# Values of the first two token blocks taken from raw x, with mean and scale applied on the way out

## The chip, the core and the metric

The kernel runs on one core of a Trainium2 chip. The metric is the device time of one execution in microseconds (us); it is given as the median of several executions. Engines are named as in the profile: PE is TensorE (PEld its weight loads), DVE is VectorE, ACT is ScalarE, POOL is GpSimd, SP is SyncE, whose queue here only issues DMAs.

## What is computed

A layer norm of x (2048 tokens, 512 features), then two branches on the normalised tokens, added to x: a sliding-window attention (32 heads of 16, window 256) and a bilinear feed-forward of width 1792.

```python
x = A_x
xn = (x - mean(x)) / sqrt(var(x) + 1e-5)
q, k, v = split(xn @ wqkv)                      # 32 heads of 16
scores = q @ k.T / 4, masked to 0 <= i - j < 256
attn = softmax(scores) @ v @ wo
mlp = ((xn @ w_gate) * (xn @ w_up)) @ w_down
return x + attn + mlp
```

All inputs and the output are bfloat16.

## The kernel before

The tokens are cut into 4 chunks (T = 0 to 3) of 512, and each chunk into 4 blocks (b) of 128. Everything stays in SBUF: the weights are loaded once at the start, and only x comes in and the result goes out.

The order of all engines' instructions is written by a planner inside the kernel, when the program is built. `run` keeps a clock for TensorE (`now`) and one for each other engine (`free`). Steps of VectorE, ScalarE and GpSimd are `op`s with a duration for each engine that may do them, a list of what they wait for, and a rank. TensorE's work is a list `A` of dense groups (four products of one bank of PSUM, mostly), a list `B` of down projections, the score batches (76 of them), and the value groups of the attention (16). `choose` takes among the first four entries of `A` (`WINDOW`) the one that can begin first; a change of tile shape costs `SWITCH`, and a transpose (`turn`) that is due within 0.4 is preferred:

```python
t = max(t, free[0][0], now)
t += SWITCH * (d.mode != self.mode) + SWITCH * (d.mode == "C" and self.mode == "D")
t -= 0.5 * (d.name.startswith("turn") and t <= now + 0.4)
```

Before the first score, an `op` with a rank above zero is held back by `HOLD` against others. Times such as `land`, `wv`, `wk`, `wq` are when a load is expected. These times only decide the order; on the chip each instruction waits for semaphores.

PSUM has eight banks: four (`S`) hold the scores of a batch, four (`M0` to `M3`) rotate among all other products. An evacuation (a copy from PSUM to SBUF) gives its bank back.

The start, chunk 0, is `first_chunk`. The prologue issues the loads on two queues, SP's and ACT's, and 42 filler matmuls (`keep_busy`, L204). For each block the statistics follow on VectorE (L598, L600), the root on ScalarE (L607), the reciprocal (L610) and the normalisation (L280) on VectorE; then TensorE transposes the block (`turn`, L631), an engine copies the transpose to `xnT` (L208 on ScalarE or L210 on VectorE), and keys, queries (L646) and values (L698, `add_v`) are projected from it. The statistics of block 1 are in two halves, the second one after block 0's normalisation. Values of a block are 16 products of 128x256 in two column tiles, one for each lane of 64 tokens. Keys go out in two copies (L291 or L289), queries in one.

After the start, chunks 1 to 3 get their transposes by DMA (L684), while scores (L222), exponentials (L505), masks (L231, L237), attention values (L252) and gate, up, down and output products (L214) alternate on TensorE. The last block's sum is made in two halves of 256 columns (`add_down`): the first goes out on SP's queue, the second, in a bank of `S`, on ACT's.

Of the kernel before, what the change touches and what calls it, by code (L numbers as in the profile page):

```python
# [36 lines left out]
class Dense:  # L37


    def __init__(self, name, mms, deps, emit, evac, mode="D"):  # L40
        self.name, self.mms, self.deps, self.emit, self.evac, self.mode = name, mms, deps, emit, evac, mode


# [43 lines left out]
class Kernel:  # L87
# [2 lines left out]
    PACE = 2.9  # L90
    SHARE = 1.0
    FEED = 0.1
    HOLD = 0.2

    def __init__(self, live=True):
        self.live = live
# [4 lines left out]
    def open(self, ctx, tc, x, wqkv, wo, wg, wu, wd, out):  # L101
        self.tc, self.nc = tc, tc.nc
        self.x_d, self.out_d = x.flatten_outer_dims(), out.flatten_outer_dims()
        self.w_d = dict(qkv=wqkv, o=wo, g=wg, u=wu, d=wd)
        self.F = wg.shape[1]

        def pool(name, bufs, **kw):
            return ctx.enter_context(tc.tile_pool(name=name, bufs=bufs, **kw))

        c = self.const = pool("const", 1)  # L110
        self.work, self.few = pool("work", 3), pool("few", 2)
        psum = pool("psum", 1, space=bass.MemoryType.PSUM)
# [24 lines left out]
        self.eps = c.tile([128, 1], F32, name="eps")  # L137
        self.own = c.tile([128, 2], F32, name="own")
        self.mhalf = c.tile([128, 4], F32, name="mhalf")
        self.masks = c.tile([128, 5, 64], I16, name="masks")  # L140
        self.S = psum.tile([128, 4, 512], F32, name="S")
        self.M = [psum.tile([128, 512], F32, name=f"M{i}") for i in range(4)] + [self.S[:, 3, :]]

    def prologue(self):
        nc = self.nc
# [3 lines left out]
        def load(eng, dst, src):  # L149
            eng.dma_start(out=dst, in_=src)  # L150

        def qkv(eng, lo, k0, k1):
            load(eng, self.Wqkv[:, k0:k1, lo:lo + 512], w["qkv"][:, k0:k1, lo:lo + 512])

        qkv(nc.sync, 1024, 0, 1)
        load(nc.scalar, self.x[:, 0, :], xv[:, 0, :])
        load(nc.sync, self.x[:, 1, :], xv[:, 1, :])
        qkv(nc.scalar, 1024, 2, 4)
        qkv(nc.sync, 1024, 1, 2)
        qkv(nc.scalar, 512, 2, 4)  # L160
        qkv(nc.sync, 512, 0, 2)
        load(nc.sync, self.x[:, 2, :], xv[:, 2, :])
# [6 lines left out]
            if lo == 0:  # L169
                load(nc.sync, self.x[:, 4:8, :], xv[:, 4:8, :])  # L170
        load(nc.sync, self.x[:, 8:NT, :], xv[:, 8:NT, :])
        for f, g in ((0, 7), (7, 14)):
            load(nc.sync, self.Wd[:, f:g], w["d"][:, f:g])
        load(nc.sync, self.Wo[:], w["o"])
        for _ in range(4):
            nc.sync.drain()

        c = self.const
        nc.gpsimd.memset(self.ident[:], 0.0)
# [2 lines left out]
        nc.gpsimd.memset(self.mhalf[:], -0.5)  # L182
        warm = c.tile([128, 1], F32, name="warm")
        nc.vector.memset(warm[:], 0.0)
        nc.vector.memset(self.eps[:], 1e-5)
        nc.scalar.activation(out=warm[:], in_=warm[:], func=ACT.Sqrt)
        self.warm = warm
# [5 lines left out]
        nc.vector.tensor_copy(out=self.own[:, 1:2], in_=podd[:])  # L193
        nc.vector.tensor_scalar(out=self.own[:, 0:1], in0=podd[:], scalar1=0, scalar2=None, op0=ALU.is_equal)
        nc.gpsimd.memset(self.V[0][:, :, :, 16:18], 1.0)
        self.keep_busy(42, 0)

# [80 lines left out]
    def i_apply(self, t, cols=slice(0, 512)):  # L278
        w, b = t // 4 % 2, t % 4
        self.nc.vector.tensor_scalar(out=self.xn[b][:, cols], in0=self.x[:, t, cols], scalar1=self.mv[w][:, b, 0:1],  # L280
                                     scalar2=self.rs[w][:, b:b + 1], op0=ALU.subtract, op1=ALU.mult)

    def i_keys(self, e, T, c, lane, in_, blocks=slice(0, 8)):

# [10 lines left out]
    def run(self):  # L295
        if self.live:
            self.prologue()
        self.now, self.mode = 4.8, "D"
# [127 lines left out]
    def do(self, at, kind, what):  # L426
# [9 lines left out]
            self.do_values(at)  # L436
        elif kind == "DA":
            d = self.A.pop(what)
            i = self.take_bank()
            o = self.pe(at, d.mms * MM, d.name)  # L440
            if self.live:
                d.emit(i)
# [139 lines left out]

    def first_chunk(self):

        land = (3.45, 3.9, 7.2, 9.6)
        wv, wk, wq = 5.4, 6.6, 9.2
        nc = self.nc
        roots = []
        for b in range(4):
# [13 lines left out]
            for n in range(halves):  # L603
# [3 lines left out]
            s = self.op(f"sq{b}", {"A": (0.24, 0.25)}, [s], lambda e, b=b: nc.scalar.activation(  # L607
                out=self.ve[:, b:b + 1], in_=self.mv[0][:, b, 1:2], func=ACT.Sqrt, bias=self.eps[:]), rank=0)
            roots.append(s)
            s = self.op(f"rs{b}", {"V": (0.15, 0.16)}, [s], lambda e, b=b: nc.vector.reciprocal(  # L610
                out=self.rs[0][:, b:b + 1], in_=self.ve[:, b:b + 1]), rank=0)
# [11 lines left out]
        for n in (1, 2):  # L623
            last = self.op("ones", {"G": (0.26, 0.33)}, [last], lambda e, n=n: self.nc.gpsimd.memset(
                self.V[n][:, :, :, 16:18], 1.0), rank=9)
        for b in range(4):
            tok = slice(128 * b, 128 * b + 128)

            def turn(i, ks, b=b):
                for k in ks:  # L630
                    self.nc.tensor.transpose(self.psT(i)[:, k, :], self.xn[b][:, 128 * k:128 * k + 128], self.ident[:])  # L631
                if b == 0:
                    self.keep_busy(2 * ks[0], 3)

            def turned(o, i, ks, b=b, tok=tok):
                took = {"A": (0.48, 0.6), "V": (0.31, 0.41)} if len(ks) == 4 else {"A": (0.27, 0.38)}
# [35 lines left out]
            self.add(f"q0b{b}", 4.4, [("xnT", 0, b), wq], lambda i, f=project: f(i, 0), q_out)  # L672

    def norms(self, T):
        w = T % 2
# [14 lines left out]
    def add_v(self, T, b, land=0.0):  # L690
# [14 lines left out]
            self.frees(x, i)  # L705
            self.at_["V", T, b] = x

        x = [("xnT", T, b)] if T + b else [("xnT", 0, 0, 0), ("begun", 0, 0, 2)]
# [50 lines left out]
    def add_down(self, T, b):  # L759
# [82 lines left out]
```

The softmax here doesn't subtract the row's maximum and nothing guards it: scores larger than these inputs give would overflow.

## Time and profile before

| | |
|---|---|
| median of 5 executions | 265.86 us (265.63 to 266.27) |
| the profiled execution | 265.63 us |
| its span, first to last instruction | 263.7 us |
| TensorE busy | 256.4 us (97%) |
| VectorE, ScalarE, GpSimd busy | 187.7, 167.7, 119.6 us |
| first value products of block 0 (L698) | 6.34 us after the span's start |
| values of blocks 1 to 3 | from 17.60 us |
| first scores (L222) | 17.27 us |
| last attention values (L252) | 245.18 us |
| last output's DMA issued | 261.22 us |

The busy time of TensorE includes the tail of each product and its overlap with the next, so it is not its rate; the spacing of products is taken from groups of them. A row of the timeline gives start, length, engine, line, operation, and in brackets how long the engine sat idle before it and what ended that.

### The profile page before, as it was taken

The numbers are of one execution on the slowest core, as the hardware profiler recorded it, in microseconds if no ns is written. First come the engines' busy times: TensorE is split into PE (matmuls) and PEld (weight loads), VectorE is DVE, ScalarE is ACT, GpSimd is POOL, SyncE is SP. The second block draws the span as 40 slices with busy tenths as digits, with TensorE's granted clock in tenths as the row PEclk, the third lists the DMA queues.
The fourth block names the chain that finished last, engine by engine and source line by source line (L and its number), as shares of the span: only waits on it lengthen the run. The fifth ranks groups of instructions, "written<-read, shape, count | busy, mean of one in ns | idle before, by whom it ended". The sixth has DMA issues, their size and how long they took to land.

```text
span 263.7 us, 7965 instructions
## 1 busy us (share of the span) xinstructions
PE 256.4 (97%) x3420; PEld 131.9 (50%) x3456; DVE 187.7 (71%) x363; ACT 167.7 (64%) x127; POOL 119.6 (45%) x272
## 2 busy tenths in 40 slices
PE   8999999999999999999999999999999999999995
PEld 7974444553535353465544453536535444544562
DVE  4789886969994438798897548786955449787504
ACT  3777576769677677577777766675786765674000
POOL 1047655455465554618165645437073645427000
PEclk9999999999999999999999999999999999999999
DMA  6999910000004000000002300000000000000002
GB/s 214 380 374 349 222 23 1 2 2 1 2 3 102 20 22 24 0 2 2 2 0 53 73 22 20 2 4 0 2 2 22 21 22 22 0 2 0 2 2 81
DMA packets 17251, 13.88 MB, mean 53 GB/s; under 512 B 7104, under 2 KB 17216, under 8 KB 17216
## 3 DMA queue, kind: packets, MB, share of 16 engines
q1 hardware_dynamic: 16384, 12.65, 17.9%
q10 hardware_dynamic: 832, 0.72, 0.9%
q8 instruction: 27, 0.44, 0.7%
q14 instruction: 8, 0.07, 0.1%
HBM read 9.70 MB, written 2.10 MB: 45 GB/s over the span
## 4 chain that ended last, share of the span: by engine, by line
PE 94%; DMA 2%; issue 1%; DVE 1%; ACT 0%
PE M L214 68%; PE S L222 10%; PE M L252 7%; PE M L698 6%; PE M L646 3%; DMA x<-in_A_x_dram 1%; DMA out_dram<-xn 1%; PE M L631 1%; PE S L214 1%; DVE xn L792 1%; DVE st L598 0%; DVE xn L280 0%; ACT ve L607 0%; PE M L204 0%; DVE mv L600 0%
## 5 line engine op out<-in xcount | busy, mean ns | idle before, releaser
L505 ACT ACTIVATE P<-S 128x2048 bf16<-128x2048 f32 x76 | 140.9, 1854 | 56.2 <-PE S L222 48.7
L231 POOL TENSOR_SCALAR_AFFINE_SELECT P<-P 64x256 bf16<-64x256 bf16 (+1 forms) x248 | 112.5, 456 | 106.8 <-ACT P L505 92.2
L214 PE MATMUL M<-xnT,Wg 128*128 128x512 bf16 x219 | 57.4, 380 | 0.3
L214 PE MATMUL M<-xnT,Wu 128*128 128x512 bf16 x213 | 56.6, 380 | 0.4
L214 PE MATMUL M<-Wd,hT 128*128 128x512 bf16 (+1 forms) x214 | 50.2, 373 | 1.4 <-issue 1.3
L750 DVE TENSOR_TENSOR hT<-M,gsb 128x512 bf16<-128x512 f32 x56 | 38.3, 683 | 7.3 <-PE M L214 7.0
L214 PEld LDWEIGHTS <-hT 128*128 128x128 bf16 x238 | 21.6, 98 | 23.2 <-issue 1.9
L214 PEld LDWEIGHTS <-Wg 128*128 128x128 bf16 x224 | 20.5, 98 | 24.9 <-issue 2.3
L210 DVE CAST gsb<-M 128x512 bf16<-128x512 f32 x41 | 28.1, 684 | 6.4 <-PE M L214 6.1
L214 PEld LDWEIGHTS <-Wu 128*128 128x128 bf16 x224 | 20.3, 98 | 24.6 <-issue 2.4
L222 PE MATMUL S<-Q,K 32*128 32x320 bf16 (+3 forms) x720 | 30.0, 254 | 0.3
L541 DVE STREAM_TRANSPOSE at<-M 128x512 f32<-128x512 f32 x32 | 21.4, 699 | 11.9 <-PE M L252 11.9
L237 DVE TENSOR_TENSOR P<-P,masks 128x512 int16<-128x512 int16 x56 | 22.3, 405 | 8.3 <-ACT P L505 8.3
L222 PEld LDWEIGHTS <-K 32*128 32x128 bf16 x720 | 12.0, 92 | 32.3 <-issue 31.1
L214 PE MATMUL M<-xnT,Wqkv 128*128 128x512 bf16 x90 | 22.6, 380 | 0.3
L792 DVE TENSOR_TENSOR y<-M,x 128x512 bf16<-128x512 f32 x12 | 8.3, 688 | 17.8 <-PE M L214 17.6
L252 PE MATMUL M<-P,V 64*17 64x320 bf16 (+4 forms) x1440 | 19.5, 252 | 0.0
L252 PEld LDWEIGHTS <-V 64*17 64x17 bf16 x1440 | 17.1, 86 | 3.0 <-issue 1.1
L291 DVE TENSOR_SCALAR K<-M,own 128x512 bf16<-128x512 f32 x21 | 15.1, 743 | 2.6 <-PE M L214 1.9
L214 PE MATMUL M<-Wo,OT 128*128 128x512 bf16 (+1 forms) x60 | 15.5, 373 | 0.5 <-issue 0.5
L698 PE MATMUL M<-Wqkv,xnT 128*64 128x256 bf16 x256 | 15.5, 274 | 0.0
L698 PEld LDWEIGHTS <-xnT 128*64 128x64 bf16 x256 | 13.4, 110 | 1.9 <-issue 1.6
(53 smaller groups left out, 149.9 us busy)
## 6 DMA issues: line engine op xcount, KB each, us to landing
Wg<-in_B_w_gate_dram SPq DMA_DIRECT2D x2, 896.0 KB, 9.6
Wu<-in_B_w_up_dram SPq DMA_DIRECT2D x2, 896.0 KB, 11.4
Wd<-in_B_w_down_dram SPq DMA_DIRECT2D x2, 896.0 KB, 13.3
out_dram<-y SPq DMA_DIRECT2D x12, 128.0 KB, 1.7
x<-in_A_x_dram SPq DMA_DIRECT2D x1, 1024.0 KB, 13.6
Wqkv<-in_A_wqkv_dram ACTq DMA_DIRECT2D x2, 256.0 KB, 4.4
Wqkv<-in_A_wqkv_dram SPq DMA_DIRECT2D x1, 512.0 KB, 5.4
x<-in_A_x_dram SPq DMA_DIRECT2D x1, 512.0 KB, 10.4
```

Source lines behind the costliest of these rows:

```text
L210: self.nc.vector.tensor_copy(out=out, in_=in_)
L214: self.nc.tensor.matmul(ps, lhsT=a, rhs=b, start=first and n == 0, stop=last and n == len(pairs) - 1)
L222: self.nc.tensor.matmul(self.S[:, e, 64 * at:64 * (at + m)], lhsT=self.K[U % 3][rows, c, j].rearrange("p l t -> p (l t)"), rhs=self.Q[T % ...
L231: self.nc.gpsimd.affine_select(out=v, in_=v, pattern=[[0, 4], [0, n], [sign, 64]], base=0, fill=0.0, compare_op=ALU.is_gt if kind else ALU ...
L237: self.nc.vector.tensor_tensor(out=v, in0=v, in1=m, op=ALU.bitwise_and)
L252: self.nc.tensor.matmul(banks[lane][32 * e:32 * e + 17, 64 * q:64 * (q + m)], lhsT=self.V[U % 3][rows, j, 4 * c + e, 0:17], rhs=P[rows, e, ...
L291: self.nc.vector.tensor_scalar(out=out, in0=in_, scalar1=own, scalar2=None, op0=ALU.mult)
L505: ex = self.op(f"exp{g}", {"A": (took + 0.06, took + 0.18)}, [o], lambda e: self.nc.scalar.activation(out=P[:, :, 0:hi], in_=self.S[:, :, ...
L541: t = self.op(f"tr{v}", {"V": (0.63, 0.71)}, [o] + ts, lambda e, par=par: nc.vector.transpose(out=self.at[:, :, par, :], in_=self.M[banks[ ...
L698: self.nc.tensor.matmul(self.M[i][64 * lane:64 * lane + 64, 256 * jj:256 * jj + 256], lhsT=self.xnT[T % 2][:, k, tok], rhs=w[:, lane], sta ...
L750: x = self.op(f"u{T}.{f}", {"V": PSUM_COPY["V"]}, [o, ("gate", T, f)], lambda e: self.nc.vector.tensor_tensor(out=self.hT[T % 2][:, f, :], ...
L792: self.nc.vector.tensor_tensor(out=keep["y"][:, cols], in0=self.M[i][:, cols], in1=self.x[:, t, cols], op=ALU.add)
```

## The change

1. Blocks 0 and 1 of x are transposed as they are loaded (`raw0`, `raw1`), into banks of `S`, with 2 and 14 filler matmuls behind them. ScalarE or VectorE copies the transposes to `xnT[1]`, which is free until chunk 1. Three of the four copies come after block 0's root on ScalarE.
2. Products of this raw x with the value weights (32 of them) go into two banks of `S`; products of a tile of -1 with the value weights (8 of them) give minus the column sums in a third one. They come in two parts of 20, `v01a` for the first half of the features and `v01b` for the second.
3. Later, at a low rank, the column sums are copied to SBUF, mean and reciprocal root are copied to the partitions of each lane (`rj`), VectorE adds mean times minus the column sum (`scalar_tensor_tensor`), and ScalarE multiplies by the reciprocal root into `V[0]`.
4. Values of blocks 0 and 1 are no longer projected from normalised tokens. Keys of chunk 0 wait for the start of `v01b`; the first scores wait for these values, as they use the same banks. Block 0's transposes lose their filler.
5. The reciprocal root is written over the variance. `HOLD` is 0.3 in place of 0.2, the planner's clock starts at 3.6 in place of 4.8, and 27 fillers stand in place of 42.
6. Loads: block 1 of x comes first on SP's queue; the first half of the value weights is one load instead of two; `Wd` is loaded in three pieces instead of two. Two drains on SP and four on VectorE take the place of four on SP.
7. The last block's sum is split into 320 and 192 columns instead of 256 and 256.

```diff
-        self.M = [psum.tile([128, 512], F32, name=f"M{i}") for i in range(4)] + [self.S[:, 3, :]]
+        self.M = [psum.tile([128, 512], F32, name=f"M{i}") for i in range(4)] + [self.S[:, e, :] for e in (3, 0, 1, 2)]
...
-        qkv(nc.sync, 1024, 0, 1)
         load(nc.scalar, self.x[:, 0, :], xv[:, 0, :])
         load(nc.sync, self.x[:, 1, :], xv[:, 1, :])
+        qkv(nc.sync, 1024, 0, 2)
         qkv(nc.scalar, 1024, 2, 4)
-        qkv(nc.sync, 1024, 1, 2)
...
-        for f, g in ((0, 7), (7, 14)):
+        for f, g in ((0, 5), (5, 10), (10, 14)):
             load(nc.sync, self.Wd[:, f:g], w["d"][:, f:g])
         load(nc.sync, self.Wo[:], w["o"])
+        for _ in range(2):
+            nc.sync.drain()
         for _ in range(4):
-            nc.sync.drain()
+            nc.vector.drain()
...
+        nc.gpsimd.memset(self.minus[:], -1.0)
...
-        self.keep_busy(42, 0)
+        self.keep_busy(27, 0)
...
-        deps = {("S", g - 1), ("Pfree", g - self.PBUFS)}
+        deps = {("S", g - 1), ("Pfree", g - self.PBUFS)} | ({("raw values", 0), ("raw values", 1)} if g == 0 else set())
...
-        land = (3.45, 3.9, 7.2, 9.6)
-        wv, wk, wq = 5.4, 6.6, 9.2
+        land = (3.5, 3.5, 7.6, 9.6)
+        wv, wk, wq = 5.4, 7.1, 9.2
...
-            at = len(self.A) - 2 if b else 0
+            at = len(self.A) - 2 if b else 3
...
-            self.add_v(0, b, wv)
-            self.add(f"k0b{b}", 4.4, [("xnT", 0, b), wk], lambda i, f=project: f(i, 512), k_out)
+            if b > 1:
+                self.add_v(0, b, wv)
+            self.add(f"k0b{b}", 4.4, [("xnT", 0, b), wk, ("values",)], lambda i, f=project: f(i, 512), k_out)
...
-            halves = [(slice(0, 256), {}, MM / 2), (slice(256, 512), {"bank": 4}, MM / 2)]
+            halves = [(slice(0, 320), {}, MM * 0.625), (slice(320, 512), {"bank": 4}, MM * 0.375)]
```

The new function, called from `first_chunk` ahead of its loop over blocks:

```python
def first_values(self, land, wv):
    raw = self.xnT[1]
    csum = self.P[6].bitcast(F32)[:, 0, :]
    vraw = self.at.rearrange("p a b c -> p (a b c)")
    for b in range(2):
        tok = slice(128 * b, 128 * b + 128)

        def turn(i, b=b):
            for k in range(4):
                nc.tensor.transpose(self.psT(i)[:, k, :], self.x[:, b, 128 * k:128 * k + 128], self.ident[:])
            self.keep_busy((2, 14)[b], 3)

        def turned(o, i, b=b, tok=tok):
            for n in range(2):
                ks = slice(2 * n, 2 * n + 2)
                deps = [o] + ([("sq", 0)] if b + n else [])
                self.at_["raw", b, n] = self.op(f"raw{b}", {"A": (0.27, 0.38), "V": (0.20, 0.29)}, deps, lambda e, ks=ks: self.copy(
                    e, raw[:, ks, tok], self.psT(i)[:, ks]), rank=0.2)

        self.add(f"raw{b}", 1.1, [land[b]], turn, turned, "D", 4 + b)

    def emit(i, ks):
        W = self.Wqkv[:, :, 1024:1536].rearrange("p k (h l d) -> p k l h d", l=2, d=16)
        for k in ks:
            for lane in range(2):
                nc.tensor.matmul(self.M[4][64 * lane:64 * lane + 64, 0:256], lhsT=self.minus[:], rhs=W[:, k, lane], ...)
        for b in range(2):
            for k in ks:
                for jj in range(2):
                    tok = slice(128 * b + 64 * jj, 128 * b + 64 * jj + 64)
                    for lane in range(2):
                        nc.tensor.matmul(self.M[6 + b][64 * lane:64 * lane + 64, 256 * jj:256 * jj + 256],
                                         lhsT=raw[:, k, tok], rhs=W[:, k, lane], ...)

    def evac(o, i):
        self.at_["values",] = o.start
        late = ("xnT", 0, 2)
        c = self.op("csum", {"V": (0.33, 0.41), "A": (0.3, 0.38)}, [o, late], lambda e: self.copy(
            e, csum, self.M[4][:, 0:256]), rank=5)
        for b in range(2):
            def stats(e, b=b):
                for j in range(2):
                    for lane in range(2):
                        self.copy(e, self.rj[b][64 * lane:64 * lane + 64, j, :], self.mv[0][64 * j:64 * j + 64, b, :])

            r = self.op(f"rj{b}", {"V": (0.5, 0.55), "A": (0.8, 0.85)}, [("rs", b), late], stats, rank=5)
            x = c
            for j in range(2):
                x = self.op(f"vm{b}", {"V": (0.36, 0.42)}, [c, r, x], ...)   # vraw = csum * mean + products
                v = self.op(f"V0.{b}", {"A": (0.32, 0.4)}, [x], ...)         # V[0] = vraw * reciprocal root
            self.at_["V", 0, b] = self.at_["raw values", b] = v

    raws = [("raw", 0, 0), ("raw", 0, 1), ("raw", 1, 0)]
    self.add("v01a", 4.9, raws + [wv - 0.35], lambda i: emit(i, (0, 1)), lambda o, i: self.at_.update({("v01a",): 0.0}), "C", 4)
    self.add("v01b", 4.9, [("raw", 1, 1), wv, ("v01a",)], lambda i: emit(i, (2, 3)), evac, "C", 4)
```

More of the change, by code (lines that the diff above doesn't have):

```diff
@@ L37, with __init__ @@
 class Dense:
-    def __init__(self, name, mms, deps, emit, evac, mode="D"):
+    def __init__(self, name, mms, deps, emit, evac, mode="D", bank=None):
+        self.bank = bank
         self.name, self.mms, self.deps, self.emit, self.evac, self.mode = name, mms, deps, emit, evac, mode
@@ L92 @@
     FEED = 0.1
-    HOLD = 0.2
+    HOLD = 0.3
     def __init__(self, live=True):
@@ L141, in open @@
         self.S = psum.tile([128, 4, 512], F32, name="S")
-        self.M = [psum.tile([128, 512], F32, name=f"M{i}") for i in range(4)] + [self.S[:, 3, :]]
+        self.M = [psum.tile([128, 512], F32, name=f"M{i}") for i in range(4)] + [self.S[:, e, :] for e in (3, 0, 1, 2)]
+        self.rj = some("rj", 2, [128, 2, 2], F32)
+        self.minus = c.tile([128, 64], BF16, name="minus")
     def prologue(self):
@@ L280, in i_apply @@
         self.nc.vector.tensor_scalar(out=self.xn[b][:, cols], in0=self.x[:, t, cols], scalar1=self.mv[w][:, b, 0:1],
[L281 removed]
+                                     scalar2=self.rs[w][:, b:b + 1] if t > 3 else self.mv[0][:, b, 1:2], op0=ALU.subtract, op1=ALU.mult)
     def i_keys(self, e, T, c, lane, in_, blocks=slice(0, 8)):
@@ L297, in run @@
             self.prologue()
-        self.now, self.mode = 4.8, "D"
+        self.now, self.mode = 3.6, "D"
         self.free = {"V": 3.0, "A": 3.4, "G": 3.0, "S": 6.0}
@@ L438, in do @@
             d = self.A.pop(what)
-            i = self.take_bank()
+            i = self.take_bank() if d.bank is None else d.bank
             o = self.pe(at, d.mms * MM, d.name)
@@ L609, in first_chunk @@
             roots.append(s)
+            self.at_["sq", b] = s
             s = self.op(f"rs{b}", {"V": (0.15, 0.16)}, [s], lambda e, b=b: nc.vector.reciprocal(
-                out=self.rs[0][:, b:b + 1], in_=self.ve[:, b:b + 1]), rank=0)
+                out=self.mv[0][:, b, 1:2], in_=self.ve[:, b:b + 1]), rank=0)
+            self.at_["rs", b] = s
             parts = 2 if b == 0 else 1
@@ L625, in first_chunk @@
                 self.V[n][:, :, :, 16:18], 1.0), rank=9)
+        self.first_values(land, wv)
         for b in range(4):
@@ L631, in turn @@
                     self.nc.tensor.transpose(self.psT(i)[:, k, :], self.xn[b][:, 128 * k:128 * k + 128], self.ident[:])
-                if b == 0:
-                    self.keep_busy(2 * ks[0], 3)
             def turned(o, i, ks, b=b, tok=tok):
-                took = {"A": (0.48, 0.6), "V": (0.31, 0.41)} if len(ks) == 4 else {"A": (0.27, 0.38)}
+                took = {"A": (0.48, 0.6), "V": (0.31, 0.41)} if len(ks) == 4 else {"A": (0.27, 0.38), "V": (0.20, 0.29)}
                 ks = slice(ks[0], ks[-1] + 1)
@@ L669, in first_chunk, with evac @@
                                             lambda o, i, f=turned, ks=ks: f(o, i, ks)))
-            self.add_v(0, b, wv)
-            self.add(f"k0b{b}", 4.4, [("xnT", 0, b), wk], lambda i, f=project: f(i, 512), k_out)
+            if b > 1:
+                self.add_v(0, b, wv)
+            self.add(f"k0b{b}", 4.4, [("xnT", 0, b), wk, ("values",)], lambda i, f=project: f(i, 512), k_out)
             self.add(f"q0b{b}", 4.4, [("xnT", 0, b), wq], lambda i, f=project: f(i, 0), q_out)
+    def first_values(self, land, wv):
+        nc = self.nc
+        if self.live:
+            raw = self.xnT[1]
+            csum = self.P[6].bitcast(F32)[:, 0, :]
+            vraw = self.at.rearrange("p a b c -> p (a b c)")
+        for b in range(2):
+            tok = slice(128 * b, 128 * b + 128)
+            def turn(i, b=b):
+                for k in range(4):
+                    nc.tensor.transpose(self.psT(i)[:, k, :], self.x[:, b, 128 * k:128 * k + 128], self.ident[:])
[9 more added lines that the diff above has]
+            W = self.Wqkv[:, :, 1024:1536].rearrange("p k (h l d) -> p k l h d", l=2, d=16)
+            for k in ks:
+                for lane in range(2):
+                    nc.tensor.matmul(self.M[4][64 * lane:64 * lane + 64, 0:256], lhsT=self.minus[:], rhs=W[:, k, lane],
+                                     start=k == 0, stop=k == 3, tile_position=(0, 64 * lane), skip_group_check=True)
+            for b in range(2):
+                for k in ks:
+                    for jj in range(2):
+                        tok = slice(128 * b + 64 * jj, 128 * b + 64 * jj + 64)
+                        for lane in range(2):
+                            nc.tensor.matmul(self.M[6 + b][64 * lane:64 * lane + 64, 256 * jj:256 * jj + 256],
+                                             lhsT=raw[:, k, tok], rhs=W[:, k, lane], start=k + jj == 0, stop=k + jj == 4,
+                                             tile_position=(0, 64 * lane), skip_group_check=True)
+        def evac(o, i):
+            self.at_["values",] = o.start
[5 more added lines that the diff above has]
+                    for j in range(2):
+                        for lane in range(2):
+                            self.copy(e, self.rj[b][64 * lane:64 * lane + 64, j, :], self.mv[0][64 * j:64 * j + 64, b, :])
+                r = self.op(f"rj{b}", {"V": (0.5, 0.55), "A": (0.8, 0.85)}, [("rs", b), late], stats, rank=5)
+                x = c
+                for j in range(2):
+                    cols = slice(256 * j, 256 * j + 256)
+                    x = self.op(f"vm{b}", {"V": (0.36, 0.42)}, [c, r, x], lambda e, b=b, j=j, cols=cols: nc.vector.scalar_tensor_tensor(
+                        out=vraw[:, 512 * b + 256 * j:512 * b + 256 * j + 256], in0=csum, scalar=self.rj[b][:, j, 0:1], in1=self.M[6 + b][:, cols],
+                        op0=ALU.mult, op1=ALU.add), rank=5)
+                    v = self.op(f"V0.{b}", {"A": (0.32, 0.4)}, [x], lambda e, b=b, j=j, cols=cols: nc.scalar.activation(
+                        out=self.V[0][:, 2 * b + j, :, 0:16], in_=vraw[:, 512 * b + 256 * j:512 * b + 256 * j + 256].rearrange("p (h d) -> p h d", d=16),
+                        func=ACT.Copy, scale=self.rj[b][:, j, 1:2]), rank=5)
+                self.at_["V", 0, b] = self.at_["raw values", b] = v
+        raws = [("raw", 0, 0), ("raw", 0, 1), ("raw", 1, 0)]
+        self.add("v01a", 4.9, raws + [wv - 0.35], lambda i: emit(i, (0, 1)), lambda o, i: self.at_.update({("v01a",): 0.0}), "C", 4)
+        self.add("v01b", 4.9, [("raw", 1, 1), wv, ("v01a",)], lambda i: emit(i, (2, 3)), evac, "C", 4)
@@ L706, in evac @@
             self.at_["V", T, b] = x
-        x = [("xnT", T, b)] if T + b else [("xnT", 0, 0, 0), ("begun", 0, 0, 2)]
+        x = [("xnT", T, b)]
         self.add(f"v{T}.{b}", 4, x + [land] + self.ring(T, 2)[:1 if T == 3 else 0], emit, evac, "C")
```

## The prediction

> **What bounds the kernel now.** I read the page first (busy shares and the chain that ended last), then that chain in order of time for the first 16 us, then the timeline of the start, the turn into attention and the end, and last the busy times by stretch.
>
> ```profile
> span 263.7 us, 7965 instructions
> ...
> PE 256.4 (97%) x3420; PEld 131.9 (50%) x3456; DVE 187.7 (71%) x363; ACT 167.7 (64%) x127; POOL 119.6 (45%) x272
> ...
> PE 94%; DMA 2%; issue 1%; DVE 1%; ACT 0%
> ```
>
> TensorE is busy for 97% of the span and makes 94% of the chain. So only three things can move the time: how much TensorE has to do, how early it starts without a pause, and what follows its last product. The chain's first steps show where the unbroken stretch begins:
>
> ```profile
> 3.70 0.71 DVE st L598
> ...
> 5.17 0.36 DVE xn L280
> ...
> 5.58 0.54 PE M L631 x4
> 6.12 0.23 PE M L204 x4
> 6.35 1.05 PE M L698 x16
> 7.40 0.04 issue
> 7.45 0.40 PE M L631 x4
> 7.84 1.79 PE M L646 x32
> ```
>
> L631 is a transpose of normalised tokens, L698 the values, L646 keys and queries, L204 filler. Before 7.45 us TensorE does only block 0's transposes and values that anyone needs; from 7.45 on it hardly stops. What starts the stretch, and where the other values lie, is in the timeline:
>
> ```profile
> 0.84 4.64 PE L204 MATMUL M<-const-bfloat16-1.0 128*128 128x128 bf16 x42 [0.84 <-PEq L826]
> ...
> 6.97 0.41 DVE L280 TENSOR_SCALAR xn<-x,mv,rs 128x512 bf16<-128x512 bf16 x1
> ...
> 7.44 0.23 PEld L631 LDWEIGHTS <-xn 128*128 128x128 bf16 x4 [0.31 <-DVE xn L280]
> ...
> 9.63 0.23 PEld L631 LDWEIGHTS <-xn 128*128 128x128 bf16 x4 [0.17 <-DVE xn L280]
> ...
> 17.60 2.81 PE L698 MATMUL M<-Wqkv,xnT 128*64 128x256 bf16 x48
> ```
>
> Block 1's transpose waits for VectorE's normalisation of block 1 (6.97), block 2's for 0.17 us. Values of blocks 1 to 3 are 48 products in one go at 17.60.
>
> **Front, the main term.** *Removed:* 16 of those 48 products. Groups of 48 take 2.74 in the chain, groups of 32 1.87 (at 116.45): 0.87 us off the path. *Added on TensorE:* 8 transposes of raw x; 32 products of raw x and 8 of the column of -1, in two parts of 20. One product costs (2.81-0.27)/47 = 0.054, so a part is 1.08; 48 by 0.054 make 2.59 and the chain has 2.74, so changing tile shape costs about 0.1, entering or leaving.
>
> Which part is free depends on the order, which the planner writes. I followed its rules for the first steps by hand, for order only. Raw transposes come first, then block 0's two half transposes, then part one, as its copies are due. Then a transpose due within 0.4 us is preferred by 0.5: block 1's lies about 0.03 inside that limit, so it goes ahead of part two; and keys of block 0 are made to wait for part two's start. On the chip:
>
> - Part one. 27 fillers at 0.107 end at 3.7, about when x lands (3.68, where the statistics start at 3.70). Two raw transposes with 16 fillers are 24 matrices more. The copies of raw x are four ScalarE steps of 128x256 (0.38 each, the row of xnT<-M 128x256), in ScalarE's waits of 0.89 and 0.96 before 4.65 and 5.90; the third ends near 5.6. Part one starts about 6.1 and ends about 7.2, still inside the wait for block 1: free.
> - Block 1's transposes: its chain of statistics is untouched, so 7.45 again.
> - Part two follows: 0.1 + 1.08 + 0.1 = 1.28 before block 0's keys, which started right after this transpose before.
> - Block 2's wait of 0.17 disappears, as its norm gets 1.28 more.
>
> Front: +1.28 - 0.87 - 0.16 = **+0.25 us**. A part of 20 with two changes of shape takes the place of 16 in a group that stays. If the hand-followed margin of 0.03 is wrong, part two goes first: 6.13 + 2.16 = 8.3, transposes till 8.6, keys at 8.6 instead of 7.67: +0.95 - 0.87 - 0.16 = -0.1.
>
> **The clock.** The 42 fillers come every 0.107 us to 5.2, the keys every 1.79/32 = 0.056 from 7.7; so the array runs at half speed for the first 4.5 us, though the granted clock is printed as 1.00 there. By this trace the 24 matrices end near 5.9 (about 15 at 0.107, the rest at 0.056). The Trainium skill, "TensorE: Matmul & The Clock Gate", Part 1, says that full speed is granted after a busy window of about 3.4 us that runs free, so that the moment varies from run to run. From work at 0.84 that puts it anywhere up to 0.84+6.8 = 7.7 (estimate from that page). The rule speaks against the change: its early work is real, 20 products now stand where 16 stood, and in that worst case the 24 matrices end at 6.3, block 0's transposes at 6.7, and part one, by the page at half speed until 7.7, at about 8.3 in place of 7.45: +0.85. By the row it costs 0. I take +0.1, the bounds being -0.2 (steadier filling helps every run) and +0.85.
>
> **VectorE and ScalarE before the first score.**
>
> ```profile
> 9.60:12.00 2.40, 2.40 (x44) 2.37 (x44) 1.97 (x5) 2.22 (x5) 0.00 (x0) 1.00 1.06 391
> 12.00:14.00 2.00, 2.00 (x40) 2.00 (x37) 1.69 (x4) 1.27 (x3) 0.98 (x5) 1.00 1.06 370
> 14.00:16.00 2.00, 1.95 (x31) 1.75 (x30) 1.46 (x3) 1.97 (x4) 1.70 (x8) 1.00 1.08 367
> ```
>
> Columns three and four after the stretch's length are TensorE and its loads, then VectorE and ScalarE. From 9.6 to 16 VectorE idles 1.28 and ScalarE 0.94 us. The change adds here: one copy of the column sums (0.42, the row y-sum 128x256 of f32), eight tiny copies of mean and scale (0.15 alone by the 128x1 CAST, 0.07 apart in a row: 0.6 to 1.2), four multiply-adds of 128x256 (no row; 0.42 by that nearest row, 0.35 to 0.7 each), and on ScalarE four scaled copies (0.38 each): about 4.4 us. Removed are a ScalarE copy of 0.60 and a later VectorE one of 0.68. TensorE's own delay of 1.28 gives both engines together 2.5 us, so 1.9 are left for gaps of 2.2, in fragments. They stand at the lowest rank, but where an engine has begun one, a key or query copy behind it waits up to 0.4, its bank of four comes free later, and TensorE waits for that. Bounds: 0, and 1.9/2 = 0.95 if no fragment can be used. I take +0.2, nearer to 0, because four banks carry 0.9 each.
>
> The first score now also waits for these values. It was at 17.27 and may come at 18 to 19; gate and up products cover that as long as banks are free. At the other end 9.03 + 2.97 us of TensorE work follow the last attention product, so a score that is 1.5 late costs nothing there.
>
> **Loads.** Without the first weight load on SP's queue, x block 1 goes first and two quarter loads of value weights are one: x block 1 earlier, where its statistics wait for VectorE anyway; the weights last needed at 6.3 before now are due by 6.1 to 6.3, with 0.2 to spare. The third piece of Wd and the moved drains: one issue of about 0.5 more and about 0.4 less on SP, whose last issue of loads ended at 23.68, ahead of the first transposing DMA at 24.78; their tiles are first read at 48.8. VectorE's four drains fall in its idle 1.76 us before 3.70. Sum 0; if SP's cover is gone, 0.5 at a queue that has 24 us. Reciprocals in the place of the variance, the larger hold (it only orders steps before the first score) and the extra memset: 0.
>
> **The end.**
>
> ```profile
> 260.06 0.60 PE L214 MATMUL S<-Wo,OT 128*128 128x256 bf16 x4
> 260.76 0.42 DVE L792 TENSOR_TENSOR xn<-S,x 128x256 bf16<-128x256 f32 x1
> 261.22 0.36 ACTq L799 DMA_DIRECT2D out_dram<-xn  x1
> ```
>
> With 320 and 192 columns the products sum to the same; the last addition falls by a quarter of the slope between 0.69 (512) and 0.42 (256): 0.07. But the addition before it grows by as much, and VectorE runs them back to back from 259.82. So 0 to -0.07. Against it stands "DMA: Bandwidth & Descriptors", Specifications: below 512 B a transfer is read, modified and written. The row is 64 KB in rows of 512 B, 1.6 us to landing; 192 columns make 384 B. By the row -0.05, by the rule up to +0.35 (estimate: twice the part above a bare latency). I take +0.05.
>
> **Sum.** 0.25 + 0.1 + 0.2 + 0.05 = +0.6. The profiled execution took 265.63 (span 263.70 and 1.93 around), the lowest of five: 266.2 for it. It lies 0.23 under the median, so the forecast is 265.86 + 0.6 = **266.5 us**. About 0.2% (0.53 us) is what a measurement of this kernel can tell from no change.
>
> **Rivals.** *Even* (0.30): copies fit their gaps and the clock rises as in this trace, only the front counts: -0.1 to +0.35, 265.8 to 266.2. For it: TensorE never starved before. Against it: VectorE and ScalarE are at 0.8 to 0.9 in just that stretch. *Faster* (0.22): part two runs ahead of block 1's transposes, and part one begins when its copies are ready, 5.65, not behind filler: -0.35; TensorE without holes also makes the early clock of the best run the rule, -0.2, and a few changes between tile shapes fewer in the rewritten order are worth 0.1 each: 265.2. It decides from the point where keys of block 0 start before 8.2. Against it: unbroken work from 5.9 only just equals today's end (the column sums and changes of shape eat what the earlier start gives). *Much slower* (0.15 of the 0.48 for slower): banks are held by the added copies, +0.95 + 0.25 = 267.1.
>
> **Chances and range.** Slower 0.48, same 0.30, faster 0.22. The range takes in the main case, the bank case and most of the faster one: 265.0 to 267.3; the likeliest case alone is 266.2 to 266.9.
>
> **What would show it.** Right: block 1's transposes still near 7.45, twenty L698-like products after them, block 0's keys at 8.7 to 9.1, the later value group with 32 products, no hole over 0.3 before the first score at 18 to 19. Wrong: keys before 8.2; TensorE holes of half a microsecond between 9 and 18; a different number of half-speed matrices; the last output landing later than 1.6 us after its issue.

## The result: slower by 0.2%, and the profile after

The changed kernel takes 266.34 us (median of 21; 265.78 to 266.75) against 265.73 for the kernel before: ratio 1.0018, 95% interval 1.0011 to 1.0025. The forecast was 266.5 us, slower. The profiled execution took 266.36 us with a span of 264.4; the one of before 265.63 with 263.7. So the loss, 0.7 us between these two executions and 0.6 between the medians, lies inside the span.

The page after, in the same rows as before:

```profile
span 264.4 us, 8021 instructions
...
PE 257.0 (97%) x3433; PEld 132.7 (50%) x3469; DVE 190.6 (72%) x373; ACT 169.4 (64%) x136; POOL 119.5 (45%) x273
...
PE 95%; issue 1%; DVE 1%; DMA 1%; ACT 0%; DVEq 0%
```

TensorE still is the chain. The chain in order of time (start, length, what) shows the new front:

```profile
3.88 0.43 PE S L694 x4
4.30 0.21 PE M L209 x2
4.52 0.44 PE S L694 x4
4.96 0.02 issue
4.98 0.38 ACT xnT L213
5.37 0.19 ACT ve L612
5.56 0.02 issue
5.58 0.17 DVE mv L616
...
7.99 0.40 PE M L639 x4
8.39 0.34 PE S L710 x4
8.73 0.87 PE S L717 x16
9.60 1.00 PE M L652 x16
```

L694 are the raw transposes, L213 on xnT a copy of raw x, L612 block 0's root, L639 the transposes of normalised blocks, L710 and L717 the column sums and products of part two, L652 keys. Part two lies between block 1's transposes and block 0's keys, as forecast. But the root is at 5.26 in the timeline, where it was at 4.65, and block 1's transposes are at 7.99 in place of 7.44. The timeline of the copy and the root shows why:

```profile
4.31 0.63 PE L694 MATMUL S<-ident,x 128*128 128x128 bf16 x4
4.39 0.18 DVE L605 BATCH_NORM_AGGREGATE mv<-st 128x2 f32<-128x6 f32 x1
...
4.98 0.38 ACT L213 ACTIVATE xnT<-S 128x256 bf16<-128x256 bf16 x1 [1.20 <-PE S L694]
5.26 0.28 ACT L612 ACTIVATE ve<-mv,eps 128x1 f32<-128x1 f32 x1
...
7.99 0.23 PEld L639 LDWEIGHTS <-xn 128*128 128x128 bf16 x4 [0.32 <-DVE xn L285]
...
9.54 1.07 PE L652 MATMUL M<-xnT,Wqkv 128*128 128x128 bf16 x16
```

In the kernel before, the same root waited for nothing but its statistics:

```profile
4.65 0.29 ACT L607 ACTIVATE ve<-mv,eps 128x1 f32<-128x1 f32 x1 [0.89 <-DVE mv L600]
```

The copy of raw block 0 needs only that block's transposes, which were done by 4.31, but it starts when those of raw block 1 have ended (4.31 + 0.63). In the trace only the last of the eight transposes raises the semaphore (the counter that other engines wait for) of TensorE. The root, whose statistics were there at 4.57, stands behind the copy in ScalarE's queue.

The added work before the first score made no hole in TensorE, that is, no pause in which it waited for a bank. The columns after the length of the stretch are TensorE, its loads, VectorE and ScalarE:

```profile
12.00:14.00 2.00, 2.00 (x39) 2.00 (x37) 1.91 (x8) 1.96 (x6) 0.00 (x0) 1.00 1.04 376
14.00:16.00 2.00, 2.00 (x40) 2.00 (x37) 2.00 (x5) 1.89 (x5) 0.00 (x0) 1.00 1.08 363
16.00:18.00 2.00, 1.95 (x27) 1.53 (x26) 1.99 (x5) 1.99 (x3) 0.00 (x0) 1.00 1.06 380
```

VectorE and ScalarE are full, TensorE too. The first score comes at 19.82 (17.27 before). And the end:

```profile
260.93 0.49 PE L219 MATMUL S<-Wo,OT 128*128 128x192 bf16 x4
261.59 0.35 DVE L866 TENSOR_TENSOR xn<-S,x 128x192 bf16<-128x192 f32 x1
261.98 0.36 ACTq L873 DMA_DIRECT2D out_dram<-xn  x1
```

The DMA view ends with the time from issue to landing:

```profile
out_dram<-xn ACTq DMA_DIRECT2D x1, 48.0 KB, 1.6
```

TensorE's last group ends at 261.42 in place of 260.66, +0.76; from its end to the issue of the last DMA it is 0.56 in both, and the DMA lands after 1.6 us in both.

The sum from the two traces: block 1's transposes +0.55; part two with its changes of tile shape 9.54 - (7.99 + 0.22) = 1.33; the later value group of 32 products -0.87; block 2's wait gone, -0.16: +0.85, and +0.76 is found at the end of TensorE's work. The remaining 0.09 is not assigned.

### The profile page after: what moved, and what is told of

Its sections match the earlier page's. It is cut to its first block, busy times and chain, and to the rows that moved or that the text cites. A ratio compares the mean times of both kernels' runs of the same rounds, so it can differ in the third digit from the quotient of the medians.

```text
span 264.4 us, 8021 instructions
## 1 busy us (share of the span) xinstructions
PE 257.0 (97%) x3433; PEld 132.7 (50%) x3469; DVE 190.6 (72%) x373; ACT 169.4 (64%) x136; POOL 119.5 (45%) x273
## 4 chain that ended last, share of the span: by engine, by line
PE 95%; issue 1%; DVE 1%; DMA 1%; ACT 0%; DVEq 0%
PE M L219 68%; PE S L227 9%; PE M L257 7%; PE M L772 5%; PE M L652 3%; PE M L209 1%; DMA out_dram<-xn 1%; PE S L219 0%; DVE xn L285 0%; DVE xn L866 0%; PE S L717 0%; PE S L694 0%; PE M L639 0%; ACT ve L612 0%; ACT xnT L213 0%
## 5 line engine op out<-in xcount | busy, mean ns | idle before, releaser
L219 PE MATMUL M<-xnT,Wg 128*128 128x512 bf16 x216 | 56.7, 380 | 0.7 <-issue 0.5
L219 PE MATMUL M<-Wd,hT 128*128 128x512 bf16 (+1 forms) x215 | 50.8, 374 | 1.4 <-issue 1.4
L296 DVE TENSOR_SCALAR K<-M,own 128x512 bf16<-128x512 f32 x25 | 18.0, 739 | 2.7 <-PE M L219 2.5
L213 ACT ACTIVATE gsb<-M 128x512 bf16<-128x512 f32 x15 | 9.0, 598 | 7.4 <-PE M L219 7.3
L219 PEld LDWEIGHTS <-Wqkv 128*128 128x128 bf16 x96 | 8.5, 98 | 10.2 <-issue 1.0
```

The costliest lines, as they stand in the source:

```text
L213: self.nc.scalar.activation(out=out, in_=in_, func=ACT.Copy)
L219: self.nc.tensor.matmul(ps, lhsT=a, rhs=b, start=first and n == 0, stop=last and n == len(pairs) - 1)
L296: self.nc.vector.tensor_scalar(out=out, in0=in_, scalar1=own, scalar2=None, op0=ALU.mult)
```

## Experiments

Ratios are to the kernel before, run on the same chip in the same set of runs.

### Raw block 0 in a tile of its own

```diff
-            self.add(f"raw{b}", 1.1, [land[b]], turn, turned, "D", 4 + b)
+            self.add(f"raw{b}", 1.1, [land[b]], turn, turned, "D", (2, 5)[b])
```

> The changed kernel with one edit: raw block 0 is transposed into bank M2, a tile of its own, instead of a bank of S; the planner's order is the same. Theory A (ScalarE's first copy of raw x waits for block 1's raw transposes only because both are in tile S, and block 0's root is queued behind that copy): the copy starts near 4.35 in place of 4.98, the root near 4.65 in place of 5.26, block 1's transposes near 7.45 in place of 7.99, total 0.5 us under the changed kernel, so 265.8 us, 0 to +0.2 against before. Rival B (the late root costs nothing because the part of twenty and fillers fill TensorE anyway, the loss is in the evacuations): the copy is early, the total stays at 266.3.

Measured: 265.92 us, ratio 1.0003 (0.9993 to 1.0012), 0.4 under the changed kernel. The timeline:

```profile
4.39 0.38 ACT L213 ACTIVATE xnT<-M 128x256 bf16<-128x256 bf16 x1 [0.61 <-PE M L694]
...
4.67 0.29 ACT L612 ACTIVATE ve<-mv,eps 128x1 f32<-128x1 f32 x1
...
7.60 0.23 PEld L639 LDWEIGHTS <-xn 128*128 128x128 bf16 x4 [0.25 <-DVE xn L285]
```

The planner's order is the same, only the bank differs, and now two of the eight transposes raise the semaphore: the copy is 0.6 earlier, the root too. Theory A holds: the shared tile is the cause of the late root. Block 1's transposes came at 7.60, not 7.45, since its own root now stands behind the copy of block 0's half transpose, which waited for fillers until 6.0. But for these 0.16 us the front of this kernel is what the prediction had worked out, and its loss can't be told from zero.

### Part two ahead of block 1's transposes

```diff
-                self.A.insert(at + n, Dense(f"turn{b}", 1.1 * len(ks) / 4, [("ap", b, n)], ...
+                self.A.insert(at + n, Dense(f"turn{b}", 1.1 * len(ks) / 4, [("ap", b, n)] + ([("values",)] if b else []), ...
```

> The changed kernel with one edit: the transposes of blocks 1 to 3 wait, in the planner, for the start of the second part of twenty, so that this part goes ahead of block 1's transposes. Theory A (order costs a hole of 0.2 and two changes of tile shape, the rest of the part has to be done anyway): keys of block 0 start near 9.2 in place of 9.54, total 0.35 us under the changed kernel, 266.0 us. Rival B (VectorE and ScalarE set the pace from 9 to 18 us, so that TensorE's earlier start is lost again to banks that come free late): 266.3, with holes of TensorE before the first score.

Measured: 266.05 us, ratio 0.9999 (0.9991 to 1.0007). Keys of block 0 started at 9.26 in place of 9.54:

```profile
9.26 1.73 PE L652 MATMUL M<-xnT,Wqkv 128*128 128x128 bf16 x28
```

TensorE had no hole before the first score. The start is 0.28 earlier, and the medians of separate sets of runs are 0.29 apart. Both fit theory A, though each interval alone is nearly as wide. The median is 0.21 over that of the kernel before in the same set (265.84) although the ratio is 0.9999; its runs fall into two groups, to which the part on the clock below returns.

### Both

```diff
-            self.add(f"raw{b}", 1.1, [land[b]], turn, turned, "D", 4 + b)
+            self.add(f"raw{b}", 1.1, [land[b]], turn, turned, "D", (2, 5)[b])
...
-                self.A.insert(at + n, Dense(f"turn{b}", 1.1 * len(ks) / 4, [("ap", b, n)], ...
+                self.A.insert(at + n, Dense(f"turn{b}", 1.1 * len(ks) / 4, [("ap", b, n)] + ([("values",)] if b else []), ...
```

> Both edits: raw block 0 in bank M2, and the second part of twenty ahead of block 1's transposes. Theory A: the two gains add, keys of block 0 near 8.7, total 0.85 us under the changed kernel, 265.5 us, 0.2 under before. Rival B (one front end limits, so the two gains are the same gain): 265.8 to 266.0.

Measured: 265.55 us, ratio 0.9992 (0.9983 to 1.0001). The timeline has the two parts back to back, and then transposes and keys:

```profile
6.14 0.41 PE L710 MATMUL S<-Wqkv,minus 128*64 128x256 bf16 x4
6.38 1.04 PE L717 MATMUL S<-Wqkv,xnT 128*64 128x256 bf16 x16
7.26 0.38 PE L710 MATMUL S<-Wqkv,minus 128*64 128x256 bf16 x4
7.48 1.04 PE L717 MATMUL S<-Wqkv,xnT 128*64 128x256 bf16 x16
8.45 0.40 PE L639 MATMUL M<-ident,xn 128*128 128x128 bf16 x4
8.68 1.95 PE L652 MATMUL M<-xnT,Wqkv 128*128 128x128 bf16 x32
```

Keys start at 8.68, 0.86 before those of the changed kernel. As theory A has it, the two gains add.

### The small parts alone, and the drains

The kernel before with the new loads, Wd in three pieces, the drains and 320/192 columns; then the drains alone; then the small parts without the drains.

```diff
         load(nc.sync, self.Wo[:], w["o"])
+        for _ in range(2):
+            nc.sync.drain()
         for _ in range(4):
-            nc.sync.drain()
+            nc.vector.drain()
```

> The kernel before with only the small parts of the change: the order and size of the first loads, Wd in three pieces, the drains, and the last block's 320 and 192 columns. Theory A: all of it costs and brings nothing, 265.7 us, within 0.1 of before. Rival C (rows of 384 B land late, or the drains shift something): +0.2 to +0.4, with the last output landing later after its issue.

> The kernel before with two drains on SP and four on VectorE in the place of four on SP, nothing else. The run with all small parts had the span of before but 2.28 us around it in place of 1.94. Theory D (the time around the span hangs on the queues' programs, here the drains): 266.1 with 2.3 around. Rival E (the loads or the last block's columns did it): 265.8 with 1.9 around.

> The kernel before with the small parts but its own four drains: loads, Wd in three, 320 and 192 columns. Theory D: 265.8 with 1.9 around the span. Rival E: 266.1 with 2.3 around it.

| kernel | us | ratio | span, median | around the span, median (lowest to highest) |
|---|---|---|---|---|
| before, beside the drains alone and the small parts without drains | 265.80 | | 263.9 | 1.94 (1.76 to 2.10) |
| all small parts | 266.09 | 1.0012 (1.0003 to 1.0020) | 263.9 | 2.28 (2.16 to 2.42) |
| drains alone | 266.13 | 1.0008 (0.9997 to 1.0020) | 263.8 | 2.29 (2.16 to 2.38) |
| small parts without drains | 265.94 | 0.9998 (0.9987 to 1.0008) | 264.0 | 1.95 (1.77 to 2.02) |
| the changed kernel | 266.34 | 1.0018 (1.0011 to 1.0025) | 264.5 | 1.90 (1.75 to 2.06) |

What is around the span is each run's time less its span. Theory A was wrong on the total and right on the span. Of rival C's two causes, the rows of 384 B are out: the last output landed in 1.6 us with them as without. Its other cause, the drains, is theory D, which holds: the drains alone carry the 0.35. It lies outside the span, where the profile shows nothing. It is shown by the time around the span; the ratio of the drains alone has an interval that still holds 1. In the changed kernel the same drains stand and the time around is 1.90, so they are not part of its loss. Why they count in one program and not in the other stays open.

### More work on VectorE

Each of the four multiply-adds issued twice.

```diff
-                    x = self.op(f"vm{b}", ..., lambda e, ...: nc.vector.scalar_tensor_tensor(
+                    def madd(e, b=b, j=j, cols=cols):
+                        for _ in range(2):
+                            nc.vector.scalar_tensor_tensor(
...
+                    x = self.op(f"vm{b}", {"V": (0.36, 0.42)}, [c, r, x], madd, rank=5)
```

> The changed kernel with each of the four multiply-adds of the values issued twice in a row: 1.9 us (4 by 0.47) more on VectorE between 13 and 20 us, where it is busy for 1.9 to 2.0 of every 2.0 us. Theory A (the added work on VectorE and ScalarE is hidden by free banks, TensorE shows no hole before the first score): the first score moves from 19.8 to 20.7 or later, the total moves by 0 to 0.2, to 266.3 to 266.5. Rival B (the cover is used up): TensorE stops for banks between 13 and 20 us, total +0.5 to +1.5.

Measured: 268.30 us (four executions), ratio 1.0092 (1.0077 to 1.0107). That is 2.0 us over the changed kernel, all of the added 1.9 within the noise, so B holds. TensorE's rows of the timeline now have holes:

```profile
17.43 1.02 PE L219 MATMUL M<-xnT,Wg 128*128 128x512 bf16 x3 [0.29 <-ACT K L294]
18.29 1.03 PE L219 MATMUL M<-xnT,Wu 128*128 128x512 bf16 x4
20.66 1.02 PE L219 MATMUL M<-xnT,Wg 128*128 128x512 bf16 x4 [1.35 <-DVE Q L215]
21.62 0.40 PE L227 MATMUL S<-Q,K 32*128 32x256 bf16 x8
```

The gate product at 20.66 waited for a bank that VectorE's copy of queries gave back.

### Less work on VectorE

```diff
-                    x = self.op(f"vm{b}", {"V": (0.36, 0.42)}, [c, r, x], ...)
-                    v = self.op(f"V0.{b}", {"A": (0.32, 0.4)}, [x], ... in_=vraw[...] ...
+                    v = self.op(f"V0.{b}", {"A": (0.32, 0.4)}, [c, r], ... in_=self.M[6 + b][:, cols] ...
```

> The changed kernel without its four multiply-adds: ScalarE scales the products straight out of PSUM, so the values lack the mean's share, and VectorE has 1.9 us less to do from 13 to 18 us. Theory A (in the changed kernel this work is just covered): the first score comes 0.8 to 1 us earlier, TensorE has no hole before or after the edit, the total does not fall: 266.3 to 266.6 (the planner's new order has two changes of tile shape more). Rival B (the added steps do cost time): 265.8 or less.

Measured: 266.57 us, ratio 1.0024 (1.0017 to 1.0032); the first score at 18.96. Taking away 1.9 us of VectorE's work brought nothing, adding as much cost all of it: the changed kernel stands near the edge where the cover ends. The first half of this is the weaker one, as the planner's order also changed; its two changes of tile shape more could hide a gain of about 0.2.

### The price of the column sums

```diff
-            for k in ks:
+            for k in ks[:1] if ks[0] == 0 else ():
                 for lane in range(2):
                     nc.tensor.matmul(self.M[4][64 * lane:64 * lane + 64, 0:256], lhsT=self.minus[:], rhs=W[:, k, lane], ...)
```

> The kernel with raw block 0 in a bank of its own and the second part ahead of block 1's transposes, where six of the eight products with the column of -1 are left out (its values lack most of the mean's share). It prices the column sums: Theory A (every product in the parts lies on TensorE's path): 6 by 0.054 = 0.3 us less, 265.25 us, keys of block 0 at 8.4 in place of 8.7. Rival B (the keys' weights, landing near 7.6, or block 1's norm set the start): no change, 265.55.

Measured: 265.28 us, ratio 0.9977 (0.9967 to 0.9987); keys of block 0 at 8.29:

```profile
8.29 2.25 PE L652 MATMUL M<-xnT,Wqkv 128*128 128x128 bf16 x32
```

From the first column product to the keys it is 2.21 us (6.08 to 8.29), against 2.54 (6.14 to 8.68) in the version with both edits: 0.33 for six products, as A has it. The totals are 0.27 apart (265.55, in another set of runs), which fits, though the two intervals just overlap. At this price all eight cost about half of what the missing block saves later (0.87).

### Fewer fillers

```diff
-                self.keep_busy((2, 14)[b], 3)
+                self.keep_busy((2, 6)[b], 3)
```

> The same kernel as the last one with all eight column products, but 6 fillers in place of 14 behind block 1's raw transposes. Theory A (the fillers end at 5.8 to 6.3, after block 0's norm, and delay the first part): the part starts near 5.9 in place of 6.14, total 0.1 to 0.25 less, 265.35. Rival B (the clock: [...]the parts run at 0.107 a pair of rows): first part slower, total +0.2 to +0.8.

Measured: 265.68 us, ratio 0.9990 (0.9982 to 0.9998). It can't be told from the version with 14 (0.9992), so neither A's gain nor B's loss is shown. In the profiled execution the first part started at 6.12, not 5.9, and the second followed at 7.49:

```profile
6.12 0.64 PE L710 MATMUL S<-Wqkv,minus 128*64 128x256 bf16 x4
6.55 1.11 PE L717 MATMUL S<-Wqkv,xnT 128*64 128x256 bf16 x16
7.49 0.38 PE L710 MATMUL S<-Wqkv,minus 128*64 128x256 bf16 x4
```

The first part took 1.37 us in place of 1.12 (6.14 to 7.26) in the version with both edits, and its four column products came every 0.107. So the slower first part that B expected is there in this one execution. More on the clock is seen by comparing fourteen fillers in the version with part two first, and in the one with one pair of column sums:

```profile
4.80 1.70 PE L209 MATMUL M<-const-bfloat16-1.0 128*128 128x128 bf16 x14
```

```profile
4.37 0.98 PE L209 MATMUL M<-const-bfloat16-1.0 128*128 128x128 bf16 x14
```

The first is 13 by 0.107 and one tail of 0.31, half speed up to the last filler's start at 6.2; the second is 13 by 0.056 and a tail of 0.25, full speed from the start at 4.4. Up to there the two programs differ only in the bank of the first raw transposes. So the moment of full speed differs between executions by about 2 us.

### Column sums in the place of fillers

Both raw blocks in banks of M, part two first, six fillers; the column products of the first two quarters as a group of their own ahead of block 0's transposes.

```diff
+        self.add("cs", 1, [4.7], lambda i: sums((0, 1)), lambda o, i: None, "C", 4)
...
-        self.add("v01a", 4.9, ...
+        self.add("v01a", 4, ...
...
-            at = len(self.A) - 2 if b else 3
+            at = len(self.A) - 2 if b else 4
```

> Both raw blocks in banks of M, second part first, 6 fillers, and the column products of the first two quarters run in the time of the fillers, as soon as their weights land (4.9): the first part is 16 products long. Theory A (TensorE's work before the keys sets the time): keys of block 0 near 8.3, total 0.3 us under the version with two edits, 265.2 us, ratio to before about 0.998. Rival B (landings and norms set the start): 265.5.

Measured: 265.44 us, ratio 0.9987 (0.9977 to 0.9997). Keys of block 0 at 8.73, not 8.3: in this execution full speed came late, and the four early products themselves ran at 5.64 to 6.15, so that block 0's transposes had to wait until 6.08. A's forecast for the keys was wrong, and its total of 265.2 too low; B's 265.5 is nearer. This version has the lowest median of those that do the whole computation, 0.13% under the kernel before and 0.9 us under the changed one, but it can't be told from the version with both edits or the one with six fillers.

## Why the prediction was right, and which of its terms were not

The total, +0.6, and the direction were right. The working was so in part: the order of the work was right, but the front cost more than forecast, and the allowances of the other terms were not seen where they were put.

**Front, +0.25 forecast, +0.85 measured.** The order was as followed by hand: part one in the hole, block 1's transposes next, part two after them at 1.33 (forecast 1.28). Right were also the 0.87 saved and block 2's wait gone. The step that failed is "its chain of statistics is untouched, so 7.45 again". The prediction put four copies of raw x into ScalarE's waits and asked whether they fit, but not when the first of them may start and what is queued behind it. That first copy stands ahead of block 0's root. It waits for a second group in the same PSUM tile, and the root behind it carries the whole chain: +0.55. So three of the signs that it named for being right did not come: block 1's transposes were at 7.99, block 0's keys at 9.54 and the first score at 19.82. In a tile of its own (first experiment) the loss is 0.03%, with an interval that holds zero and also the forecast +0.25 us (0.09%).

**The clock, +0.1 forecast for the fillers and part one; the executions point to the front instead.** In the profile after, fourteen fillers took 1.52 us, so most of them ran at half speed, and yet they ended at 6.26 behind transposes that could not start before 6.18: no loss there in this execution. But the copy ahead of the root waits for eight raw transposes, and these, with two fillers between them, took 1.25 us at half speed (3.69 to 4.94). In the version with one pair of column sums, where full speed came early, they took 0.78 (3.75 to 4.53):

```profile
3.75 0.44 PE L694 MATMUL M<-ident,x 128*128 128x128 bf16 x4
...
4.15 0.38 PE L694 MATMUL S<-ident,x 128*128 128x128 bf16 x4
```

So with an early full speed most of the +0.55 should go, about 0.47 by these rows (an estimate). The other executions agree. A mean granted clock under 1.000 goes with an early full speed in both traces that have it: those of all small parts and of the drains alone read 0.999, and their 42 fillers end at 4.86 and 4.72 in place of 5.48. (An execution at 1.000 can be an early one too, as that with one pair of column sums.) Of the 22 executions of the changed kernel that have a span on record, the 7 so marked have a median span of 264.3 and the other 15 of 264.5; with part two first, in the same shared tile, it is 263.7 for 9 and 264.2 for 12; in the kernel before 263.9 for 24 and for 107. That the shared tile makes the changed kernel depend on the clock fits all of this, but no trace of an early execution of it was kept, so it is argued and not shown. The Trainium skill, "TensorE: Matmul & The Clock Gate", Part 1, is borne out in that the moment varies (before 4.4 in one execution, after 6.2 in another). Its figure of about 0.5 us either way is too small for that, and the measurement decides.

**VectorE and ScalarE, +0.2 forecast, none seen,** with bounds of 0 and 0.95. TensorE has no hole to the first score, and less work brought nothing that can be seen beside the new order. The concern behind the upper bound was sound, though: 1.9 us of further work cost 2.0.

**The end, +0.05 forecast, 0 measured.** Below 512 B a row the Trainium skill, "DMA: Bandwidth & Descriptors", Specifications, expects a read, modify and write; 48 KB in rows of 384 B landed in 1.6 us like 64 KB in rows of 512 B. The measurement decides: no cost here. The upper bound of +0.35 had a further weakness: it rests on a bare latency for which the prediction gives no number.

**Loads, 0 forecast.** Without the drains the small parts are at 0.9998 (0.9987 to 1.0008). The drains, also put at 0, cost 0.35 in the kernel before and nothing that shows in the changed one.

So the total is better than its working, and that is luck. A front 0.6 too low was made up for by 0.35 of allowances that did not come where they were put, and by 0.24 between the terms' +0.85 and the +0.61 of the medians. Of this, 0.09 is not assigned, and 0.12 comes from comparing two traced executions, as the one of before was 0.10 faster than its median and the other 0.02 slower. Of the rivals, *even* would have been right with one line changed in the kernel (the bank). *Faster* took 0.35 from the order and an early part one; the version with both edits, which has these, is 0.29 under the kernel before, at 0.9992 with an interval that just holds 1. The further 0.3 that brought this rival to 265.2 is not seen.

## What to carry to other kernels

Work moved into a hole of the limiting engine is free only if what prepares it does not stand ahead of the chain that ends the hole. For each new step, look at the queue of its engine and ask what is behind it. Ask also what the step really waits for: here a second group in the same tile moved the start of a copy. In a kernel with one full engine, compare totals of useful work too: here two early parts of 20 products, with changes of tile shape around them, replace 32 products, so that at best a few tenths are left. And test a cover by adding as much again: a profile with three full engines does not tell whether there is 0 or 2 us of slack.

## What the runs showed of the hardware

- A ScalarE copy whose own transposes were done by 4.31 us started at 4.98, when four more transposes into another part of the same PSUM tile had ended; with a tile of its own it started at 4.39, and block 1's transposes moved from 7.99 to 7.60.
- Two drains fewer on one queue and four more on another made 0.35 us outside the span in the kernel before (2.29 in place of 1.94 around it, with no overlap between the executions run side by side) and nothing in the changed one. Among 30 executions of the kernel before in another set, one had 2.31 around it without these drains.
- The moment of full speed of TensorE came before 4.4 us in one profiled execution and after 6.2 in another with the same instructions up to there, but for one bank; the granted clock of the profile reads 1.00 over this stretch in both, so the spacing of products has to be read instead.
- A last output in rows of 384 B landed no later than one in rows of 512 B.
